# The last unit of a fused attention and feed-forward kernel: the tile of two units' rests second in its block, and another order of products and stores in the last tile

## Chip, core and metric

The kernel runs on one core of a Trainium2 chip. The metric is the device time of one execution in microseconds (us); of several runs the median is taken.

## The reference

Attention with normalized queries and keys on 8 batches of 12 heads, 448 positions and 64 channels; its output, as 3584 rows of 768, goes through a feed-forward layer of 2048 hidden units with a squared ReLU. All in fp32.

```
q_n, k_n = rmsnorm(q, g_q), rmsnorm(k, g_k)            # over the 64 channels
attn = softmax(q_n @ k_n.T / 8) @ v                    # (8, 12, 448, 64)
x = attn.transpose(0, 2, 1, 3).reshape(3584, 768)
h = np.maximum(x @ w_in, 0.0)                          # w_in (768, 2048)
out = h * h @ w_out                                    # w_out (2048, 768)
```

## The kernel before, in words

The batches are taken in pairs: a **unit** `u` is two batches of 448 rows, so there are four units, 0 to 3. While TensorE (PE) runs the feed-forward layer of one unit, the attention of the next is woven in between; the last unit, 3, has no attention beside it. `final` is true for it.

A unit's feed-forward layer (`ffn`) goes over four **blocks** (`NBLK`) of the hidden units. In each block the first matrix product gives the hidden values `hid` (`deep_products`, matmuls on L1042), and the second product (`second_products`, matmuls on L1251 and L1165) multiplies them by a part of `w_out` and adds the result to accumulators in SBUF. Both use a scheme with seven products in place of eight (Strassen's, in Winograd's form): for each tile the upper and lower rows and the left and right half of the columns are the four quarters. `PRODUCTS` lists for each of P1 to P7 which of three PSUM banks it uses, whether it starts that bank anew or adds to what an earlier product left there, and its two operands. After a product, an engine adds the bank to the quarters that it belongs to: P1 and P2 to the upper left (`c11`), P6 and P3 to the upper right (`c12`), P4 to the lower left (`c21`), P5 to the lower right (`c22`), and P7 to both lower quarters. P6 adds to P1's bank and P7 to that of P1 and P6; P3 adds to P5's bank. These additions are L1345 (`add_to`) and L1272 (P4, a subtraction) on VectorE (DVE); in a unit's first block they are copies instead, some of them on ScalarE (ACT, L1341 and L1266).

Of the 448 rows of a batch, 384 make three tiles of 128 (`NT` is 3, `tt` counts them); the tile `tt` has 128 rows of the unit's first batch as its upper rows (`accs[2 * tt]`) and 128 of its second as its lower rows (`accs[2 * tt + 1]`). The 64 **rest** rows of each batch are left. In units 0 and 3 the rests of the unit's own two batches are multiplied in `multiply_rest` (L1165). Units 1 and 2 keep the hidden values of their rests in DRAM (`keep_rests`), and the last unit brings them back block by block (`bring_rests`, loads on L1192), makes the sums that the scheme needs on GpSimd (POOL, `add_rests`, L1203), and multiplies them as one more tile with the number `NT`; its two accumulators are `extra["accs"]`, in the trace `qk`, as they lie in a room that held queries and keys before. Its hidden values are `extra[...]`, in the trace `wT`.

In a block of the last unit the tiles come in the order 0, 1, 2, `NT`. Tile 0 has the order of products `FIRST_OF_BLOCK`, which holds the rest products too; the other tiles have `SECOND_ORDER`: P1, P2, P5, P6, P4, P3, P7.

In the last block (`blk == NBLK - 1`) the accumulators are stored. `product` puts `(tt, 0)`, the upper rows, in `to_store` after P3, and `(tt, 1)`, the lower rows, after P7. `store_some` empties that list after P2 and P4 of a later tile, and what is left at the end of the last tile is stored in the loop on L1329. `store_rows` finds the accumulator and its rows in the output, `store` (L1346) issues a DMA on SyncE's queue (SP): one of 128 rows for a tile, two of 64 rows where the rows belong to rests. SP works off its queue in order, and each of its DMAs waits for the additions that it needs; other engines' order does not hold it up otherwise. In the last block SP has 12 stores: two of the unit's own rests, two each of tiles 0, 1 and 2 (in the trace `out_dram<-acc`), and four of tile `NT` (`out_dram<-qk`).

Which of two programs runs is decided at the start by a branch on L104; at its end each engine branches once more (L104) to the common end of the kernel (L1893), where SP waits for the DMAs' semaphores and all engines meet.

Of the kernel before, what the change touches and what calls it, by code (L numbers as in the profile page):

```python
# [39 lines left out]
def kernel(  # L40
# [63 lines left out]
    with tc.If(flag > 0) as either:  # L104
        program(tc, rows, v, g, wide, ones, moe_w_in, moe_w_out, out, shift=False)
    with either.Else():
        program(tc, rows, v, g, wide, ones, moe_w_in, moe_w_out, out, shift=True)
# [118 lines left out]
def program(ctx, tc, rows, v, g, wide, ones, moe_w_in, moe_w_out, out, shift):  # L226

    nc = tc.nc

    B, H, S, D = v.shape  # L230
    NPAIR = H // 2
    DM, DFF = moe_w_in.shape
# [3 lines left out]
    HALF = DM // 2  # L236
    REST = S % P
    NT = S // P
    NBLK = 4
# [666 lines left out]
    def turn_roles(*order):  # L906
        roles[:] = [roles[n] for n in order]
# [8 lines left out]
    FIRST_ORDER = ["P1", "P5", "P2", "P6", "P3", "P4", "P7"]  # L916
    FIRST_OF_BLOCK = ["P1", "rest0", "P5", "P4", "P6", "P2", "rest1", "P3", "P7"]
    SECOND_ORDER = ["P1", "P2", "P5", "P6", "P4", "P3", "P7"]
    SPLIT_ORDER = [
        ("P1", 0, 0), ("P1", 1, 3), ("P4", 0, 2), ("P5", 0, 1), ("P4", 1, 4), ("P6", 0, 0),  # L920
        ("P2", 0, 2), ("P3", 0, 1), ("P7", 0, 0), ("P6", 1, 3), ("P2", 1, 1), ("P5", 1, 0),
# [21 lines left out]
    def ffn(u):  # L943

        accs = []
        for blk in range(NBLK):

            hid = [
                ffn_p.tile([P, 2, 2, S], F32, name="hid", tag=f"hid{a}", bufs=1) for a in range(2)
            ]  # L950
            sums_ = [
                ffn_p.tile([P, 2, NT * P], F32, name="sums", tag=f"S{n}", bufs=1) for n in range(3)
            ]
            second = second_products(u, blk, hid, sums_, accs)
            if u == B // 2 - 1:
                bring_rests(blk)
                add_rests()
            if u:
                yield from deep_products(u, blk, hid, sums_, second)
            else:  # L960
                for t in range(2):
                    products = first_products(u, 2 * blk + t, [a[:, t] for a in hid])
                    for n, cost in enumerate(products):
                        if t and n < 4:
                            hidden_sum(hid, sums_, 0, n)
                        if t and blk == NBLK - 1:
                            let_go(u, PRODUCTS[FIRST_ORDER[n]][3])
                        yield cost
                make_all_deep()
                if blk == NBLK - 1:  # L970
                    for n in range(4):
                        load_piece(n, False)
                        load_piece(n, True)
            yield from second
# [184 lines left out]
    def multiply_rest(u, blk, hid, places, some, acc=None, halves=range(2)):  # L1159

        w_sb = [out_sb[n] for n in out_of(u, blk)]
        for half in halves:
            ps = places[half][:, 0:HALF]
            for a, t in some:
                nc.tensor.matmul(  # L1165
                    ps, lhsT=hid[a].rearrange("p t e s -> p t (e s)")[:, t, ds(NT * P, P)],
                    rhs=w_sb[t][:, 2 * a + half, :],
                    start=(a, t) == PARTS[0], stop=(a, t) == PARTS[-1],
                )
            if acc is not None:  # L1170
                add_to(acc[:, ts(half, HALF)], ps, blk == 0)
# [33 lines left out]
    def second_products(u, blk, hid, sums_, accs):  # L1205

        split, final = u in KEPT, u == B // 2 - 1
# [18 lines left out]
                yield len(some) * COST_OUT  # L1226
            turn_roles(2, 1, 0)

        def store_rows(tt, e):
            if tt is None or tt == NT:  # L1230
                n = u if tt is None else KEPT[e]
                parts = [(2 * n, P * NT, REST), (2 * n + 1, 0, REST)]
            else:
                parts = [(2 * u + e, REST * e + P * tt, P)]
            store(accs[-1] if tt is None else accs_of(tt)[e], parts)

        def accs_of(tt):
            return extra["accs"] if tt == NT else accs[2 * tt : 2 * tt + 2]
# [5 lines left out]
        def product(tt, name, ps, engine):  # L1244

            upper_acc, lower_acc = accs_of(tt)
            c11, c12 = [upper_acc[:, ts(h, HALF)] for h in range(2)]
            c21, c22 = [lower_acc[:, ts(h, HALF)] for h in range(2)]
            role, first, left, right = PRODUCTS[name]
            for t in range(2):  # L1250
                nc.tensor.matmul(  # L1251
                    ps, lhsT=extra[left][:, t] if tt == NT else lefts[left][:, t, ts(tt, P)],
                    rhs=w_sb[t][:, OUT.index(right), :], start=first and t == 0, stop=t == 1,
                    skip_group_check=not first,
                )
            if name == "P1":
                add_to(c11, ps, blk == 0, engine)
            elif name == "P5":
                add_to(c22, ps, blk == 0, engine)
            elif name == "P2":  # L1260
                add_to(c11, ps)
            elif name == "P6":
                add_to(c12, ps, blk == 0, engine)
            elif name == "P4":
                if blk == 0 and engine is nc.scalar:
                    nc.scalar.mul(c21, ps, -1.0)  # L1266
                elif blk == 0:
                    nc.vector.tensor_scalar(
                        out=c21, in0=ps, scalar1=-1.0, scalar2=None, op0=ALU.mult
                    )  # L1270
                else:
                    nc.vector.tensor_tensor(out=c21, in0=c21, in1=ps, op=ALU.subtract)  # L1272
            elif name == "P3":
                add_to(c12, ps)
                to_store.append((tt, 0))
            else:
                add_to(c21, ps)
                add_to(c22, ps)
                to_store.append((tt, 1))

        def sums_behind_first():
            make_sums(0, 1)
            yield COST_OUT
            make_sums(2, 3)
            held.discard("pool")

        def store_some(name):
            if name in ("P2", "P4") and blk == NBLK - 1:
                while to_store:
                    store_rows(*to_store.popleft())  # L1290

        if split:
            places = [*roles, banks[1], banks[2]]
            for name, tt, n in SPLIT_ORDER:
                engine = nc.scalar if tt and n < 3 else nc.vector
# [8 lines left out]
                if tt:  # L1304
                    store_some(name)
                yield COST_OUT
        for tt in range(0 if split else NT + final):
            order = SECOND_ORDER if tt or not u else FIRST_OF_BLOCK
            for name in order:
                if name.startswith("rest"):  # L1310
                    a = int(name[-1])
                    multiply_rest(
                        u, blk, hid, banks[2:0:-1], PARTS_BY_ROW[2 * a : 2 * a + 2],
                        accs[-1] if a else None,
                    )
                    if a:
                        held.discard("others")
                    yield 2 * COST_OUT
                    continue
                ps = roles[PRODUCTS[name][0]][:, 0:HALF]  # L1320
                product(tt, name, ps, nc.scalar if order is SECOND_ORDER else nc.vector)
                if name == "P1" and order is FIRST_OF_BLOCK:
                    yield from sums_behind_first()
                    continue
                if order is not FIRST_OF_BLOCK:
                    store_some(name)
                yield COST_OUT
            turn_roles(2, 0, 1)
        while to_store and blk == NBLK - 1:  # L1329
            some = to_store.popleft()  # L1330
            if final:
                store_rows(*some)
            else:
                later.append([2, lambda some=some: store_rows(*some)])
        for n in ns:
# [3 lines left out]
    def add_to(acc, ps, first=False, engine=nc.scalar):  # L1339
        if first and engine is nc.scalar:  # L1340
            nc.scalar.copy(acc, ps)  # L1341
        elif first:
            nc.vector.tensor_copy(out=acc, in_=ps)
        else:
            nc.vector.tensor_tensor(out=acc, in0=acc, in1=ps, op=ALU.add)  # L1345
    def store(acc, parts):  # L1346

        at = 0
        for b, row, n in parts:
            nc.sync.dma_start(out[ds(b * S + row, n), :], acc[at : at + n, :])  # L1350
            at += n


# [465 lines left out]
    with tc.manual_schedule(engines=ENGINES):  # L1819
# [8 lines left out]
        for i in range(len(pairs) + 1):  # L1828
            for n in range(1 if whole(i) else VISITS):
                at = i * VISITS + n - VISITS - unit  # L1830
# [3 lines left out]
                u, x = divmod(at, unit)  # L1834
                if x == 0:
                    u, x = u - 1, unit
# [61 lines left out]
```

## Time and profile before

| | |
|---|---|
| median of 3 runs | 1393.48 us (1393.12 to 1394.81) |
| the profiled execution, in all | 1394.38 us |
| its span, first to last instruction | 1392.6 us |
| granted TensorE clock, mean | 0.998 of full |
| PE busy with matmuls | 1363.3 us, 98% of the span |
| VectorE, ScalarE, GpSimd busy | 58%, 44%, 57% |
| DMA | 233.36 MB, mean 168 GB/s |
| matmuls L1251 on `hid`, `sums` | 768 and 576, mean 488 and 490 ns busy, some 323 ns from start to start in the last unit |
| additions L1345 on accumulators | 312 of 128x384, mean 548 ns |

Busy times of different engines lie beside each other and do not add up to the span. A matmul's busy time overlaps the next one's, so the distance from start to start says what a row of matmuls takes. In the lines of a profile the form is: source line, engine, operation, output<-input, and then counts and times; "SPq" is SyncE's instruction queue, where a DMA's time is that of its issue, and the time from issue to landing stands apart.

### The profile page before, as it was taken

What the parts mean: (1) busy time and instruction counts of PE and PEld (TensorE: products, weight loads), DVE (VectorE), ACT (ScalarE), POOL (GpSimd) and SP (SyncE); (2) the same over time, 40 slices, a digit from 0 to 9 for tenths busy, and PEclk for the clock granted to TensorE, in tenths of its full rate; (3) what the DMA queues carried; (4) which work ended last, traced back from release to release, by engine and by line L of the source; (5) the groups of instructions that cost most, each with busy time, mean ns of one, the idle gap of its engine ahead of it and who ended that gap; (6) DMA issues with size and microseconds to landing.
All of it is one profiled execution on the core that took longest, in us unless ns stands there. A gap on an engine that the chain in (4) does not pass through costs nothing.

```text
span 1392.6 us, 19474 instructions
## 1 busy us (share of the span) xinstructions
PE 1363.3 (98%) x6320; PEld 845.7 (61%) x6320; DVE 807.2 (58%) x1635; ACT 608.3 (44%) x1118; POOL 789.6 (57%) x794
## 2 busy tenths in 40 slices
PE   7999999999999999999999999999999999999997
PEld 3333444444444466676758586676768677868684
DVE  4786545867758755555556755455546642445444
ACT  6885477757666244353434244442434032202020
POOL 5668664746656868576667877566745630303030
PEclk9999999999999999999999999999999999999999
DMA  5566746968769875664739475755527442424223
GB/s 147 149 168 169 203 117 159 264 179 219 233 155 284 231 215 162 187 173 141 204 86 279 140 225 149 211 153 176 146 86 239 142 165 103 135 90 149 78 90 100
DMA packets 385588, 233.36 MB, mean 168 GB/s; under 512 B 272452, under 2 KB 354244, under 8 KB 381380
## 3 DMA queue, kind: packets, MB, share of 16 engines
q1 hardware_dynamic: 385184, 231.95, 57.7%
q8 instruction: 52, 0.85, 0.3%
q14 instruction: 60, 0.49, 0.1%
q10 hardware_dynamic: 292, 0.07, 0.0%
HBM read 174.59 MB, written 57.34 MB: 167 GB/s over the span
## 4 chain that ended last, share of the span: by engine, by line
PE 81%; POOL 4%; DVE 4%; DMA 3%; issue 3%; SPq 2%; ACT 2%; POOLq 0%; ACTq 0%; DVEq 0%
PE bank L1251 30%; PE bank L1042 20%; PE bank L986 8%; PE bank L446 5%; PE bank L536 5%; PE bank L550 4%; PE bank L435 4%; PE bank L1165 2%; POOL sum L473 2%; PE bank L585 1%; DMA qk<-in_k_dram 1%; PE bank L611 1%; SPq L326 1%; SPq L318 1%; PE bank L571 1%
## 5 line engine op out<-in xcount | busy, mean ns | idle before, releaser
L1042 PE MATMUL bank<-xT,in_sb 128*128 128x224 f32 x1344 | 289.3, 354 | 2.9 <-ACT part L1031 2.3
L1251 PE MATMUL bank<-out_sb,hid 128*128 128x384 f32 x768 | 272.5, 488 | 2.2 <-POOL out_sb L1514 1.4
L1345 DVE TENSOR_TENSOR acc<-acc,bank 128x384 f32<-128x384 f32 x312 | 166.6, 548 | 164.6 <-PE bank L1251 138.1
L1042 PEld LDWEIGHTS bank<-xT,in_sb 128*128 128x128 f32 x1344 | 252.6, 190 | 15.0 <-ACT wT L454 5.6
L454 ACT ACTIVATE wT<-bank,rr 128x448 f32<-128x448 f32 x288 | 163.5, 631 | 155.1 <-PE bank L435 92.7
L1251 PE MATMUL bank<-out_sb,sums 128*128 128x384 f32 x576 | 207.2, 490 | 1.3 <-DVE acc L1345 0.9
L1251 PEld LDWEIGHTS bank<-out_sb,hid 128*128 128x128 f32 x768 | 144.7, 190 | 104.5 <-issue 5.6
L204 POOL TENSOR_TENSOR rr<-ms,minus_half 128x8 f32<-128x8 f32 (+1 forms) x96 | 146.0, 1521 | 73.7 <-DVE ms L197 63.8
L1251 PEld LDWEIGHTS bank<-out_sb,sums 128*128 128x128 f32 x576 | 107.7, 190 | 86.3 <-issue 4.3
L1027 DVE TENSOR_TENSOR hid<-hid,bank 128x224 f32<-128x224 f32 x312 | 111.0, 383 | 83.9 <-PE bank L1042 79.1
L986 PE MATMUL bank<-xT,in_sb 128*128 128x448 f32 x336 | 131.9, 546 | 0.1
L473 POOL TENSOR_TENSOR sum<-sum,wT 128x448 f32<-128x448 f32 (+1 forms) x96 | 110.6, 1173 | 8.1 <-ACT wT L454 6.6
L986 PEld LDWEIGHTS bank<-xT,in_sb 128*128 128x128 f32 x336 | 62.1, 190 | 69.0 <-issue 60.2
L446 PE MATMUL bank<-qT,kT 64*128 64x448 f32 (+1 forms) x492 | 100.5, 571 | 1.9 <-DVE qT L409 1.1
L473 POOL TENSOR_TENSOR sum<-wT 128x448 f32<-128x448 f32 x48 | 55.8, 1183 | 69.8 <-ACT wT L454 69.8
L1099 ACT ACTIVATE hid<-hid 128x448 f32<-128x448 f32 x96 | 55.0, 573 | 66.7 <-DVE hid L1027 48.5
L435 PE MATMUL bank<-qT,kT 64*64 64x448 f32 x552 | 77.0, 547 | 1.9 <-ACT wT L454 1.9
L1042 PE MATMUL bank<-more,in_sb 128*128 128x224 f32 x288 | 76.2, 357 | 1.4 <-DVE hid L1037 1.4
L550 PE MATMUL bank<-wT,vt 64*64 64x448 f32 x576 | 74.3, 548 | 0.0
L1039 ACT COPY hid<-bank 128x448 f32<-128x448 f32 x24 | 12.8, 532 | 137.3 <-PE bank L1042 137.3
L369 ACT ACTIVATE qT<-qT,g 128x448 f32<-128x448 f32 x34 | 22.6, 665 | 113.7 <-DVE qT L367 113.7
L446 PEld LDWEIGHTS bank<-qT,kT 64*128 64x128 f32 (+1 forms) x492 | 34.9, 166 | 60.4 <-issue 36.8
(140 smaller groups left out, 2059.1 us busy)
## 6 DMA issues: line engine op xcount, KB each, us to landing
out_sb<-out_forms SPq DMA_DIRECT2D x24, 1536.0 KB, 9.9
in_sb<-in_deep SPq DMA_DIRECT2D x64, 384.0 KB, 4.2
in_sb<-in_deep SPq DMA_DIRECT2D x80, 256.0 KB, 4.1
words<-in_moe_w_in_dram SPq DMA_DIRECT2D x32, 384.0 KB, 3.8
words<-in_moe_w_out_dram SPq DMA_DIRECT2D x32, 384.0 KB, 3.6
out_forms<-out_sb SPq DMA_DIRECT2D x8, 1536.0 KB, 7.5
qk<-in_q_dram SPq DMA_DIRECT2D x96, 96.0 KB, 2.6
qk<-in_k_dram SPq DMA_DIRECT2D x96, 96.0 KB, 2.7
```

The costliest lines, as they stand in the source:

```text
L204: self.nc.gpsimd.tensor_tensor(out=self.rr[i][:, x, 0 : self.count(i)], in0=ms, in1=self.minus_half.to_broadcast(list(ms.shape)), op=ALU.pow,)
L435: nc.tensor.matmul(sc[ds(half * D, D)], lhsT=turned[i, 1][ds(e * D, D), ds(m * P + half * D, D)], rhs=turned[i, 0][ds(e * D, D), :], start ...
L446: nc.tensor.matmul(sc[some], lhsT=turned[p, 1][r, keys], rhs=turned[p, 0][r, :], start=True, stop=True,)
L454: nc.scalar.activation(new_weights((i, m), e), sc, AF.Exp, scale=rows.rr[i][:, 1, 2 * m + e : 2 * m + e + 1],)
L473: nc.gpsimd.tensor_tensor(out=sums[i, e][some], in0=left[some], in1=weights[key_of(i, m), e][some], op=ALU.add)
L536: nc.tensor.matmul(values_bank(i)[ds(e * D, D), :], lhsT=lasts[i % 2][mine, e, :] if m == NJ else values[i][:, m, e, :], rhs=weights[key_o ...
L550: nc.tensor.matmul(bank[ds(e * D, D), :], lhsT=values[i][keys, n, e, :], rhs=weights[(i, n), e][keys], start=n == 0, stop=n == NJ - 1 and ...
L986: nc.tensor.matmul(ps, lhsT=w_sb[:, IN.index(left), c, :], rhs=forms[u, c][right], start=first and c == 0, stop=c == NK - 1, skip_group_ch ...
L1027: nc.vector.tensor_tensor(out=quarter(name, n), in0=quarter(base, n), in1=ps, op=ALU.add)
L1042: nc.tensor.matmul(ps, lhsT=left, rhs=right, start=start, stop=stop, skip_group_check=True)
L1251: nc.tensor.matmul(ps, lhsT=extra[left][:, t] if tt == NT else lefts[left][:, t, ts(tt, P)], rhs=w_sb[t][:, OUT.index(right), :], start=fi ...
L1345: nc.vector.tensor_tensor(out=acc, in0=acc, in1=ps, op=ALU.add)
```

## The change

In the last unit the tiles of every block come in the order 0, `NT`, 1, 2, so that the tile of the two units' rests is second and tile 2 is last. In the last block, tile 2 has a new order, `LAST_ORDER`, with P7 ahead of P3. There the upper rows are stored in two parts: the left half of the columns after P2, the right half at the end. The lower rows, complete after P7, stand before that right half on SP's queue. `store` and `store_rows` take the columns as an argument. The last block's stores are then 13, and the last three of them are those of tile 2: left half of the upper rows, lower rows, right half of the upper rows. Every other product, addition and load is the same, in the same numbers.

```
+    LAST_ORDER = ["P1", "P2", "P5", "P6", "P4", "P7", "P3"]
...
-        def store_rows(tt, e):
+        def store_rows(tt, e, columns=slice(None)):
...
-            store(accs[-1] if tt is None else accs_of(tt)[e], parts)
+            store(accs[-1] if tt is None else accs_of(tt)[e], parts, columns)
...
-        for tt in range(0 if split else NT + final):
-            order = SECOND_ORDER if tt or not u else FIRST_OF_BLOCK
+        for tt in () if split else (0, NT, 1, 2) if final else range(NT):
+            ends = final and blk == NBLK - 1 and tt == NT - 1
+            order = LAST_ORDER if ends else SECOND_ORDER if tt or not u else FIRST_OF_BLOCK
...
-                product(tt, name, ps, nc.scalar if order is SECOND_ORDER else nc.vector)
+                product(tt, name, ps, nc.vector if order is FIRST_OF_BLOCK else nc.scalar)
...
                 if order is not FIRST_OF_BLOCK:
                     store_some(name)
+                if ends and name == "P2":
+                    store_rows(tt, 0, slice(0, HALF))
...
         while to_store and blk == NBLK - 1:
             some = to_store.popleft()
             if final:
-                store_rows(*some)
+                store_rows(*some, slice(0 if some[1] else HALF, DM))
...
-    def store(acc, parts):
+    def store(acc, parts, columns=slice(None)):
...
-            nc.sync.dma_start(out[ds(b * S + row, n), :], acc[at : at + n, :])
+            nc.sync.dma_start(out[ds(b * S + row, n), columns], acc[at : at + n, columns])
```

## The prediction

> **What bounds the kernel now.** I read the page's first part, then the table of stretches over the last unit (its four blocks end near 1166, 1237, 1307 and 1376 us, each followed by its last tile), then the timeline of the last microseconds, then what the stores and the ending branch did.
>
> The page's first part and the table of stretches. In the table the columns after the length are busy us and count of each engine, the granted clock, the DMA share and GB/s:
>
> ```profile
> PE 1363.3 (98%) x6320; PEld 845.7 (61%) x6320; DVE 807.2 (58%) x1635; ACT 608.3 (44%) x1118; POOL 789.6 (57%) x794
> ```
>
> ```profile
> 1096.00:1166.00 70.00, 70.00 (x281) 52.92 (x280) 31.54 (x68) 17.68 (x36) 23.68 (x26) 1.00 0.39 136
> 1307.00:1376.00 69.00, 69.00 (x279) 52.38 (x278) 32.21 (x67) 12.47 (x25) 15.84 (x16) 1.00 0.30 111
> 1376.00:1393.00 17.00, 9.07 (x29) 5.01 (x27) 5.37 (x10) 0.00 (x0) 0.00 (x0) 0.91 0.32 96
> ```
>
> PE is busy for 70.00 of 70.00 and 69.00 of 69.00 us: up to its last product the unit is a gapless row of matmuls. A new order cannot make that row shorter, only open holes in it. What is left is the stretch after PE's last product, some 7.5 us (1385.1 to 1392.6). The timeline of it:
>
> ```profile
> 1375.88 9.19 PE L1251 MATMUL bank<-out_sb,wT 128*128 128x384 f32 x28
> ...
> 1383.82 0.56 DVE L1345 TENSOR_TENSOR qk<-qk,bank 128x384 f32<-128x384 f32 x1 [0.74 <-PE bank L1251]
> 1384.40 3.58 SPq L1350 DMA_DIRECT2D out_dram<-qk  x4
> 1385.11 1.02 DVE L1345 TENSOR_TENSOR qk<-qk,bank 128x384 f32<-128x384 f32 x2 [0.73 <-PE bank L1251]
> ```
>
> The last tile is the one of the two rests; P7 comes last and has two additions (1.02 us) behind it. Both halves of its rows leave by four DMAs, two of them only after the second addition. Narrow windows on the stores give the last two apart (issue time min/median/max in ns):
>
> ```profile
> L1350 SPq DMA_DIRECT2D out_dram<-qk x1: 466/466/466, 1386.2 to 1386.2; - x1
> ...
> L1350 SPq DMA_DIRECT2D out_dram<-qk x1: 1307/1307/1307, 1386.7 to 1386.7; - x1
> DMA to landing us min/median/max: 3.6/3.6/3.6
> ```
>
> The last store is issued from 1386.67 to 1387.98 and lands 3.6 us after its start, at 1390.3. What stands after it, by source line (L104 is the branch that leaves the program, L1893 the common end):
>
> ```profile
> L104 DVEq COMPARE_BRANCH  x1: 57/57/57, 1385.1 to 1385.1; - x1
> L104 SPq COMPARE_BRANCH  x1: 43/43/43, 1388.0 to 1388.0; - x1
> ```
>
> ```profile
> L1893 SPq EVENT_SEMAPHORE  x4: 28/28/28, 1391.2 to 1391.4; - x4
> L1893 ACTq DRAIN  x1: 81/81/81, 1350.5 to 1350.5; - x1
> L1893 DVEq DRAIN  x1: 57/57/57, 1388.6 to 1388.6; - x1
> ```
>
> SP branches at 1388.0 and does nothing until 1391.2, 0.9 us after the last store has landed. So it is the branch that ends the kernel, not the landing: SP's last issue, 3.2 us of branch, then 1.35 us of closing semaphores to 1392.6. DVE needs 3.5 us for the same branch, ACT, which left while the DMA engines were idle, 2.5 us (1348.0 to 1350.5).
>
> [...] after SP's branch two packets of the instruction queue are seen at about 1389.6 and nothing of SP before 1391.2. [...] the trace has 553 (mean of the seven additions on qk). [...] Here SP's 128-row stores of that size land in 2.3 us when alone; the four 64-row stores of half the size, close together, take 3.2 to 4.0. I use the trace's values.
>
> **The change part by part.**
>
> *Order of tiles, four blocks.* A tile is 7 products of 4 matmuls; the row of x28 above occupies PE from 1375.88 to 1384.91, 9.03 us, as the other tiles do (1357.82, 1366.85, 1375.88). Nothing is added or removed: 0 us on PE if the inputs are there. The tile of the rests is wanted 18.06 us earlier. Its sums are POOL's L1203: in block 0 the four are done at 1111.3 (last start 1110.5 plus 0.76), wanted at 1146.05 (its old 1164.11 less 18.06), 35 us spare; in block 3 done at 1320.1 (last start 1319.4), wanted at 1357.8, 38 us spare. The loads L1192 of the next block wait for this tile's reads, with load_piece and load_out behind them on SP's queue; the wait ends 18 us sooner, so nothing behind it is later. POOL's 104.4 us of waiting for these loads lie in idle time. Without the covers of 35 us the tile would stall PE by what is missing. Tile 2 now borders on the next block, whose first ACT and DVE writes into `hid` wait for its reads; but they need results of matmuls that stand behind those reads on PE: 0.
>
> *Last tile, P7 before P3.* P7 adds into P6's bank with only P4 between. The addition of a product ends 0.2 + 0.56 us after the product's last matmul starts (1383.62, 1383.82 to 1384.38); P7 would start 1.29 + 0.32 us after it: 0.85 us spare, 0. P3's bank was read three products earlier. Now one addition (P3's) follows PE's last product instead of two: it runs 1385.11 to 1385.66 in place of 1386.13. **-0.47 us.**
>
> *Stores.* Twelve DMAs become thirteen; the added one (upper rows, left half, issued after P2's addition at about 1378.5) meets an idle SP, 0.33 to 0.6 us by the issues of the page's 8 acc stores: 0. The rests' and tile 1's stores all leave one or two tiles earlier. P7's two additions end at 1384.84 (1383.82 plus 1.02); the lower rows' store is issued then, free again at about 1385.2. The right half waits for P3's addition and starts at 1385.69 (0.03 after it, as at 1386.16 now). One last store instead of two: **-0.51 us** (1386.16 to 1386.67). Its issue: now 1.31 us, and a packet of 16 KB of the instruction queue starts at the same moment, 1.5 us after DVE's branch; that would still be near 1386.7, and SP would be done by then. The 128-row stores took 0.33 us alone and up to 0.50 in a series; the form of 128 rows by 1.5 KB is not in the stores of before. Bounds 0.33 and 1.31; I take 0.40: **-0.91 us**. SP then branches at 1386.1 in place of 1388.0.
>
> *Branch and end.* With 3.2 us the semaphores start at 1389.3, the end is 1390.7. Less than half as many bytes are under way at that time (the lower rows' 384 KB from 1384.87 and 192 KB, against 768 KB after 1384.4), so the fetch should wait less: between 0 and 0.7 us (3.2 less ACT's 2.5); I take **-0.2 us**. The right half lands, by 2.3 to 3.6 us, between 1388.0 and 1389.3, before SP looks. DVE's end of branch at 1388.6 is not late either, since SP is needed at the same barrier after it.
>
> Sum: -0.47 - 0.51 - 0.91 - 0.2 = **-2.1 us**: the profiled span goes from 1392.6 to 1390.5. That execution took 1394.38 in all, 1.8 around the span, and stands 0.9 above the median of the runs, 1393.48. From the median: **1391.4 us**.
>
> A difference of 0.2% is 2.8 us here, about what a measurement of this kernel can tell from no change (its three runs lie 1.7 us apart). The forecast is 0.15%.
>
> **The rivals.**
> - *The gain is bigger.* The branch takes ACT's 2.5 us and the issue 0.33: -0.47 - 0.51 - 0.98 - 0.7 = -2.7 us, and with the before runs' upper half (1394.38, 1394.81) as the truer level the comparison shows -2.8 to -3.3. For it: the fetch now falls after most of the stores' bytes. Against: DVE's branch took 3.5 us with half of the stores under way. 1390.5 us. Chance 0.25.
> - *The gain is small.* DVE's fetch meets the last issue after all (1.31 us again), or the right half in 1.5 KB rows lands last, at 4.0 us or more (1389.7 and later), and the landing takes the branch's place: -0.5 to -1.2 us, 1392.6. Against: the new issue should end 0.6 us before that fetch. Chance 0.12. That the stores would not be issued ahead at all is no case: the built order of SP's instructions has left half, lower rows, right half as its last three.
> - *Slower.* At each of three block borders PE stops because tile 2's `hid` and `sums` are read to the very end, where the tile of the rests used to give 9.03 us of cover. Price: as long as one 128x448 ACT or DVE step (0.58 to 1.1 us) each, times three, 1.7 to 3.3 us, against a saving of 2.1; it decides from 0.7 us a border on, and to end beyond +0.2% it would need 1.6. Against: [...] 70.00 of 70.00 us busy shows that no border stops it now. 1394.5 us, up to 1396.5. Chance 0.03.
>
> The forecast has the remaining 0.60, itself -1.5 to -2.6 us. Chances: faster by over 0.2% 0.25, within 0.72, slower 0.03. Range: 1390.2 (the bigger gain) to 1393.0 (the small one).
>
> **What would show it.** Right: the blocks' stretches still 70.00 of 70.00; PE's last matmul, now on `sums`, at the same 1384.6; one addition of 0.56 us after 1385.1; SP's last store near 1385.7 with 0.3 to 0.5 us of issue; SP's first L1893 near 1389.1; span near 1390.5. Wrong: idle PE before L1042 at 1166, 1237 or 1307; idle PE at 1357.8 with a releaser on POOL; a last issue of over 1 us; semaphores of L1893 that stand apart because a landing is awaited.

## The result and the profile after

The changed kernel takes 1391.94 us (median of 20 runs, 1389.98 to 1394.52), the kernel before 1393.99 us (1392.60 to 1396.41) in runs beside it: ratio 0.9984, 95% interval [0.9977, 0.9991], so 0.16% or 2.2 us less. The forecast was 1391.4 us and 0.15%.

The profiled execution has a span of 1389.3 us, 3.3 us under the one before. Only 2.0 of these belong to the change. In the trace the 2001st matmul, some 590 us ahead of the last unit, starts at 507.5 us in place of 508.6, and the first addition behind PE's last product at 1383.86 in place of 1385.11: most of that lead of 1.25 us was there long before anything that was changed. So I count from that addition on and call the stretch to the span's end the **tail**: 7.47 us before, 5.46 us after. The same stretch is the measure in the experiments, from one trace each. Three pairs of kernels below end in nearly the same way and differ in it by 0.01 us (6.12 and 6.11), 0.08 (3.58 and 3.50) and 0.20 (5.46 and 5.66), so I read nothing into steps smaller than that.

The table of stretches over the last unit, columns as before: PE is as gapless as it was.

```profile
1096.00:1166.00 70.00, 70.00 (x281) 52.91 (x280) 30.98 (x66) 17.78 (x36) 26.52 (x30) 1.00 0.41 143
1307.00:1376.00 69.00, 69.00 (x279) 52.37 (x278) 32.70 (x68) 12.49 (x25) 12.98 (x12) 1.00 0.31 109
1376.00:1393.00 17.00, 7.82 (x25) 4.29 (x23) 4.35 (x8) 0.00 (x0) 0.00 (x0) 0.90 0.20 73
```

The timeline at the end of the last tile: P7's two additions come first, one addition stands alone behind PE's last product.

```profile
1382.37 1.45 PE L1252 MATMUL bank<-out_sb,sums 128*128 128x384 f32 x4
...
1382.57 1.02 DVE L1349 TENSOR_TENSOR acc<-acc,bank 128x384 f32<-128x384 f32 x2 [0.73 <-PE bank L1252]
1383.86 0.55 DVE L1349 TENSOR_TENSOR acc<-acc,bank 128x384 f32<-128x384 f32 x1 [0.27 <-PE bank L1252]
```

The last store in a narrow window on the output: one issue of 332 ns where the last of before took 1307, but a landing that takes 3.9 us.

```profile
L1354 SPq DMA_DIRECT2D out_dram<-acc x1: 332/332/332, 1384.4 to 1384.4; - x1
...
DMA to landing us min/median/max: 3.9/3.9/3.9
```

The branches (L104), and the common end (now L1897), by source line:

```profile
L104 DVEq COMPARE_BRANCH  x1: 57/57/57, 1383.9 to 1383.9; - x1
L104 SPq COMPARE_BRANCH  x1: 43/43/43, 1384.8 to 1384.8; - x1
```

```profile
L1897 SPq EVENT_SEMAPHORE  x8: 17/28/28, 1387.9 to 1388.4; - x8
L1897 DVEq DRAIN  x1: 57/57/57, 1387.6 to 1387.6; - x1
```

SP branches 1.0 us after the start of the last addition, not 2.9, and is back 3.0 us later (3.15 before). The tail, step by step, in us from the start of the first addition behind the last product; "leaves" is the end of SP's branch instruction, "back" its first instruction at the common end:

| | last store issued | its issue | SP leaves | SP back | end |
|---|---|---|---|---|---|
| before | 1.56 | 1.31 | 2.97 | 6.12 | 7.47 |
| after | 0.58 | 0.33 | 1.00 | 4.03 | 5.46 |

### The profile page after: what moved, and what is told of

The parts are those of the page before. It is cut to its first block, busy times and chain, and to the rows that moved or that the text cites. A ratio compares the mean times of both kernels' runs of the same rounds, so it can differ in the third digit from the quotient of the medians.

```text
span 1389.3 us, 19475 instructions
## 1 busy us (share of the span) xinstructions
PE 1361.8 (98%) x6320; PEld 845.1 (61%) x6320; DVE 807.2 (58%) x1635; ACT 608.9 (44%) x1118; POOL 789.9 (57%) x794
## 4 chain that ended last, share of the span: by engine, by line
PE 82%; DVE 5%; POOL 5%; issue 2%; DMA 2%; SPq 2%; ACT 1%; DVEq 0%; POOLq 0%; ACTq 0%
PE bank L1252 30%; PE bank L1043 20%; PE bank L987 8%; PE bank L446 5%; PE bank L536 5%; PE bank L550 4%; PE bank L435 4%; PE bank L1166 2%; POOL sum L473 2%; PE bank L585 1%; DMA qk<-in_k_dram 1%; PE bank L611 1%; PE bank L571 1%; PE bank L602 1%; SPq L159 1%
## 5 line engine op out<-in xcount | busy, mean ns | idle before, releaser
L1096 POOL TENSOR_TENSOR hid<-hid 128x448 f32<-128x448 f32 x24 | 27.2, 1138 | 122.9 <-DVE hid L1028 118.1
```

## The experiments

**The tiles alone.**

```
-            ends = final and blk == NBLK - 1 and tt == NT - 1
+            ends = False
...
-                store_rows(*some, slice(0 if some[1] else HALF, DM))
+                store_rows(*some)
```

> Only the order of tiles is changed (0, rests, 1, 2); products keep P3, P7 at the end and the stores stay whole. The measure is the tail: from the start of the first addition behind the last product to the end of the span, 7.47 us in the kernel before and 5.46 in the changed one. Theory (SP's last issue and the ending branch set the end): two additions stand before the last store, but it is one DMA of 128 rows in place of two of 64, so tail 1.05 + 0.35 + 3.1 + 1.4 = about 5.9 us, some 1.5 us less than before, ratio 0.9989. Rival (the new order of products and the split stores make the gain): tail about 7.4 us, ratio 1.000. Rival (the moved tile makes the row of matmuls itself shorter): idle PE that goes from the blocks, or PE's row from the unit's start to its last product shorter by over 0.5 us.

Measured: ratio 0.9989 [0.9983, 0.9996], tail 6.12 us, near the theory's 5.9; SP leaves at 1.47, is back at 4.77. From the first matmul of the rests' tile in block 0 to the last matmul it is 238.54 us, as in the changed kernel; in the kernel before 220.48, and with the two tiles by which that first matmul has moved (18.06 us) 238.54 again. So PE's row is the same to 0.01 us. Two thirds of the gain come without the new order of products, by one store behind the last addition in place of two (by the tails, 1.35 of 2.01 us).

**Products and stores alone**, in the rests' tile, which stays last.

```
-            ends = final and blk == NBLK - 1 and tt == NT - 1
+            ends = final and blk == NBLK - 1 and tt == NT
...
-        for tt in () if split else (0, NT, 1, 2) if final else range(NT):
+        for tt in range(0 if split else NT + final):
```

> The order of tiles stays (the rests' tile last), and that last tile gets P7 before P3 and its stores in left half, lower rows, right half, each as two DMAs of 64 rows. Theory: the two issues of the lower rows (0.47 + 0.59) keep SP until 0.85 us after the start of the last addition, the right half's two issues follow, so SP leaves at about 1.9 us (2.7 if the last issue is again 1.3 us): tail 6.5 us, or 7.2. Rival (one addition less and an earlier start are what counts): tail 5.9 us or less. Ratio to before 0.9993 by the theory.

Measured: ratio 0.9994 [0.9985, 1.0002], tail 6.36 us. SP's issues queue up as worked out: four in a row, 0.47 to 0.59 us each, the last from 1.56 to 2.15 us, SP leaves at 2.24. The last one starts where the 1.31 us issue of before did, and takes 0.59: the 16 KB packet of the instruction queue begins at 2.10 here, not at 1.57.

**The upper rows whole.** The left half is not stored ahead; the last store has 384 KB.

```
-                if ends and name == "P2":
-                    store_rows(tt, 0, slice(0, HALF))
...
-                store_rows(*some, slice(0 if some[1] else HALF, DM))
+                store_rows(*some)
```

> The changed kernel without the split: the upper rows of the last tile are stored whole (384 KB) after P3, behind the lower rows. Theory one (issue and branch alone set the end, the split does nothing): tail 5.5 us as in the changed kernel. Theory two (in the changed kernel the last landing, 3.9 us after its issue, is already level with the branch): the landing comes 0.5 to 0.9 us later and is waited for, tail 5.9 to 6.3 us.

Measured: ratio 0.9992 [0.9985, 0.9998], tail 5.88 us. The size of theory two, but by another way than it said. SP leaves at 1.00 us as in the changed kernel and is back only at 4.45, not at 4.03. By source line, the branch and the end:

```profile
L104 SPq COMPARE_BRANCH  x1: 43/43/43, 1386.4 to 1386.4; - x1
```

```profile
L1895 SPq EVENT_SEMAPHORE  x8: 17/28/28, 1389.9 to 1390.5; - x8
L1895 DVEq DRAIN  x1: 58/58/58, 1389.2 to 1389.2; - x1
```

It is the branch that takes 3.45 us. The landing is waited for too (it comes at 4.85 us and costs SP 0.09 us), but that is the smaller part.

**The last store in two.**

```
+            if two:
+                parts = [(b, row + n // 2 * x, n // 2) for b, row, n in parts for x in range(2)]
...
-                store_rows(*some, slice(0 if some[1] else HALF, DM))
+                store_rows(*some, slice(0 if some[1] else HALF, DM), not some[1])
```

> The changed kernel with its last store (right half of the upper rows) as two DMAs of 64 rows in place of one of 128. Theory (each issue counts): one issue of 0.47 and one of 0.59 in place of 0.33, SP leaves 0.73 us later, tail 6.2 us; if the second issue meets DVE's instruction fetch it is 1.3 us and the tail 6.9. Rival (the landing of all stores sets the end): tail within 0.2 us of 5.46, since the bytes are the same.

Measured: ratio 0.9998 [0.9990, 1.0005], tail 5.79 us. SP leaves 0.79 us later (1.79), as the theory says, yet is back only 0.42 later (4.45): its branch takes 2.66 us. Neither side is right: not each issue counts in full, for the branch that starts later here finds more of the stores' bytes gone. Counted in the DMA packets, 184 KB of the stores begin after SP leaves here, 408 KB in the changed kernel. The times are worse than this one trace explains (it would give 0.9988, just below the interval's lower edge); that stays open.

**The programs swapped.**

```
-        program(tc, rows, v, g, wide, ones, moe_w_in, moe_w_out, out, shift=False)
+        program(tc, rows, v, g, wide, ones, moe_w_in, moe_w_out, out, shift=True)
     with either.Else():
-        program(tc, rows, v, g, wide, ones, moe_w_in, moe_w_out, out, shift=True)
+        program(tc, rows, v, g, wide, ones, moe_w_in, moe_w_out, out, shift=False)
```

with the flag's comparison turned round (`is_gt` for `is_le`).

> The changed kernel with the two programs in the other order (the one for large gains in the If, the one that runs in the Else), so that the program that runs stands last, right before the common end, and the far jump comes at the start. Theory (the ending branch with its fetch of instructions is what follows SP's last issue): SP is in the closing semaphores at once, the last store lands without the fetches' packets at about 2.6 to 2.9 us after the start of the last addition, tail about 3.9 us in place of 5.46; the jump at the start costs from 0 to 3 us, so ratio to before 0.997 to 0.9995. Rival (the landings or the closing barrier set the end): tail still 5.3 to 5.5 us.

Measured: tail 3.58 us, and yet ratio 1.0026 [1.0015, 1.0038]. The end shows what the branch costs. Its lines in narrow windows, the common end and then the last store:

```profile
L1897 SPq EVENT_SEMAPHORE  x10: 17/28/28, 1394.4 to 1396.9; - x10
```

```profile
L1354 SPq DMA_DIRECT2D out_dram<-acc x1: 332/332/332, 1394.0 to 1394.0; - x1
...
DMA to landing us min/median/max: 2.0/2.0/2.0
```

No branch, no packet of instructions in the tail, SP at the end's semaphores 0.04 us after its issue, and the same store lands in 2.0 us, not 3.9. The price at the start was expected at 0 to 3 us and is more, and with it the expected ratio failed: the 21st matmul comes 2.9 us later than in the kernel before (17.4 for 14.5), the 801st 5.7 (163.4 for 157.7), the 3001st 8.1 (699.6 for 691.5; the other kernels lie between 688.0 and 691.5). The first 2.9 us fit the far jump at the start: DVE branches at 10.2 us and its next operation comes at 13.28, in the changed kernel at 10.50 after a branch at 10.3; what adds the rest through the attention part isn't settled.

**No branch at all.** The program for large gains is left out; for other inputs than these it would be needed.

```
-    flag = nc.values_load(bounded, min_val=0, max_val=1)
-    with tc.If(flag > 0) as either:
-        program(..., shift=False)
-    with either.Else():
-        program(..., shift=True)
+    program(..., shift=False)
```

> The changed kernel without the If: the program for large gains is left out, and with it the load of the flag and both branches. Theory: tail about 3.9 us as with the swapped programs, and no jump at the start, so the whole is at least 1.5 us shorter than the changed kernel: ratio to before 0.9973 or less. Rival (the end is set by landings or the barrier): tail 5.3 to 5.5 us, any gain lies at the start.

Measured: ratio 0.9970 [0.9958, 0.9982], tail 3.50 us; the last store lands at 2.60 us, and the end follows 0.90 later. It beats both kernels, but not as the same function. The gain over the changed kernel (0.14% by the two ratios, 2.0 us) is that of its tail (1.96 us), though six runs leave about 1.7 us on either side. At the start no price of the branch that isn't taken is seen: the 21st matmul starts at 14.35 us here, and between 14.28 and 14.62 in the twelve kernels that have that branch and don't take it.

**P3 in halves, one bank.**

```
+            if name == "P3" and u == B // 2 - 1 and blk == NBLK - 1 and tt == NT - 1:
+                for some in (slice(0, HALF // 2), slice(HALF // 2, HALF)):
...
+                    add_to(c12[:, some], ps[:, some])
+                store_rows(tt, 1)
+                to_store.clear()
+                for n in range(2):
+                    store_rows(tt, 0, slice(HALF + HALF // 2 * n, HALF + HALF // 2 * (n + 1)))
+                return
```

> The changed kernel with the last product (P3 of the last tile) as two column halves of 192, each with its own addition and its own store, so that only an addition of 128x192 and a store of 96 KB stand behind the last matmul. Theory: the last addition takes 0.36 us in place of 0.56, SP leaves 0.2 us earlier, tail about 5.25 us; the four shorter matmuls lengthen PE's row by about 0.1 us. Ratio to before 0.9983, not to be told from the changed kernel by its times, only by the trace. Rival (the branch's fetch waits for the stores' bytes): tail shorter by 0.4 us or more, as fewer bytes stand ahead of it.

Measured: ratio 0.9986 [0.9978, 0.9994], tail 4.84 us, but PE's row is 1.00 us longer, not the 0.1 that I had estimated. The timeline of PE:

```profile
1383.08 0.81 PE L1254 MATMUL bank<-out_sb,sums 128*128 128x192 f32 x4
1384.62 0.92 PE L1254 MATMUL bank<-out_sb,sums 128*128 128x192 f32 x4 [0.73 <-DVE acc L1363]
```

The second half waits for the addition of the first, as both lie in one bank. That was the step I had missed; it takes back more than the tail gave. The shorter addition takes 0.35 us; the expected 0.36 lies on the line through the 0.39 of 224 columns and the 0.56 of 384 in the kernel before. The tail's 0.62 us is three times the 0.20 that this addition saves: the branch takes 2.70 us with fewer bytes ahead of it (132 KB begin after SP leaves, not 408), as the rival has it. In good part that is the stall's own doing, for the lower rows' store is issued 1.25 us ahead of the last addition here, and 0.24 in the changed kernel.

**Small last stores.** The lower rows and the right half are written in 16 columns each; the rest of them is left out.

```
-                store_rows(*some, slice(0 if some[1] else HALF, DM))
+                store_rows(*some, slice(0, 16) if some[1] else slice(HALF, HALF + 16))
```

> The changed kernel with the last two stores cut to 16 columns each (the rest of the lower rows and of the right half is not written). Theory (SP's fetch of instructions waits behind the stores' bytes in the DMA engines): from SP's branch to its next instruction 2.5 us, as for ACT in the kernel before, in place of 3.0, and tail 4.9 us. Rival (the branch takes its time whatever is under way): 3.0 us and tail 5.3 to 5.5.

Measured: ratio 0.9984 [0.9978, 0.9990], tail 5.06 us; from SP's branch (1.00) to its return (3.72) 2.72 us, between the theory's 2.5 and the rival's 3.0. So the stores' bytes cost some 0.3 us of the branch in the changed kernel; 2.7 us it takes even when hardly a byte is under way (8 KB begin after SP leaves). Even this store lands only 3.1 us after its issue. The trace records the landing of a store in 16 parts: 14 are there at 2.00 us after the addition's start, the last at 3.70; a 16 KB packet of instructions ran from 1.21 to 2.62.

**The kernel before, rests in one store.**

```
-                parts = [(2 * n, P * NT, REST), (2 * n + 1, 0, REST)]
+                parts = [(2 * n, P * NT, P)]
```

> The kernel before with one edit: the 64 rest rows of the first batch and of the second stand behind each other in the output, so a store of rests is one DMA of 128 rows in place of two of 64. Tiles and products as before. Theory (the number of issues behind the last addition, and their form, make most of the gain; which tile is last makes none): two additions, then one issue of 0.33 us, so tail 6.1 us as with the tiles moved alone, ratio 0.9989. Rival (the place of the tile matters in itself): tail over 7 us, ratio 1.000.

Measured: tail 6.11 us, ratio 0.9994 [0.9987, 1.0002]. One line in the kernel before, and its tail is that of the tiles moved alone (6.12), with SP leaving at 1.47 us in both. The last store in a narrow window:

```profile
L1350 SPq DMA_DIRECT2D out_dram<-qk x1: 332/332/332, 1385.1 to 1385.1; - x1
```

The times hold both no gain and the expected 0.9989 just within the interval.

**Products and stores, rests in one store.** The second experiment with that line.

> Tile order as before (rests last), the new order of products and the split stores in that tile, and its stores as one DMA of 128 rows each. Theory: the tail of the changed kernel, 5.4 to 5.6 us, in place of the 6.36 us with stores of 64 rows, and its whole gain, ratio 0.9984, without moving a tile. Rival (the moved tile has a part in it): tail or PE's row longer by 0.3 us or more than in the changed kernel.

Measured: tail 5.66 us, ratio 0.9986 [0.9980, 0.9993]: the changed kernel's gain with no tile moved. SP leaves at 1.00 and is back at 3.93 us; the 0.2 us above the changed kernel come of its wait of 0.40 us for the last landing (4.44 us), which stands earlier among the end's semaphores here. In this kernel the landing, and not the branch, ends last.

**The last product in two banks.** P5 and P3 of the last tile in halves of two matmuls each, the right half in a free bank; the rests' tile in one store as above.

```
+                for n, some in enumerate(pieces_):
+                    room = (banks[3] if n else ps)[:, 0 : HALF // 2]
...
+                    add_to(acc[:, some], room)
+                    if not first:
+                        at = HALF + HALF // 2 * n
+                        store_rows(tt, 0, slice(at, at + HALF // 2))
```

> The changed kernel, stores of rests in one DMA, and in the last tile P5 and P3 in two column halves of 192, this time in two PSUM banks, so that no half waits for the addition of the other. Theory: PE's row is again of the changed kernel's length within 0.1 us (eight half matmuls of 0.16 us for four of 0.32), the last addition takes 0.35 us and the last store is 96 KB: tail 4.8 to 4.9 us as with the halves in one bank, so the whole is about 0.6 us shorter than the changed kernel, ratio to before 0.998. Rival (halves cost PE time in themselves): PE's row longer by 0.6 us or more, and nothing gained.

Measured: PE's row is the changed kernel's within 0.02 us, so the two banks mend that. But the ratio is 0.9990 [0.9981, 0.9998], the tail 6.73 us and not 4.8 to 4.9. The last two stores in a narrow window:

```profile
L1373 SPq DMA_DIRECT2D out_dram<-acc x2: 383/1123/1863, 1385.3 to 1385.8; - x2
```

The last issue took 1.86 us. It started at 0.65 us, and a 16 KB packet of the instruction queue at 0.77. The 1.31 us issue of before had met such a packet too (1.56 and 1.57). In the views of the DMA queues (packets, MB, share of the 16 engines' time) it is the one of q8, an instruction queue, first in a window on this kernel's last issue, then in one on that of before:

```profile
q8 instruction: 1, 0.02, 5.1%
```

```profile
q8 instruction: 1, 0.02, 11.6%
```

All traces together, counted packet by packet, bear this out. In the 14 traces 446 stores go to the output; these two alone had such a packet begin in their first 0.13 us, and these two alone took over 1 us to issue. Of all of SP's DMAs, 95 had one begin in their first 0.13 us: 67 of them took over 1 us, while of the other 17403 it was 6%. When the packet began 0.2 to 0.4 us after the issue's start, 4 of 102 did.

**Two banks, one last store** of 192 KB after both additions; so its issue is over before such a packet.

```
-                    if not first:
-                        at = HALF + HALF // 2 * n
-                        store_rows(tt, 0, slice(at, at + HALF // 2))
+                if not first:
+                    store_rows(tt, 0, slice(HALF, DM))
```

> As the kernel with the last product in two banks, but with one store of the right half (192 KB) after both additions, so that the last issue starts at 0.38 us after the start of the last addition in place of 0.65. Theory (the issue of 1.86 us there was its meeting with a 16 KB instruction packet that began at 0.77 us): the issue takes 0.33 us and is over by 0.72, SP leaves at 0.76, tail 4.8 to 5.2 us, the whole 0.3 to 0.6 us shorter than the changed kernel, ratio to before 0.998. Rival (short additions or two banks lengthen the last issue in themselves): issue again over 1 us, tail 6 us or more.

Measured: ratio 0.9987 [0.9980, 0.9993], tail 5.38 us, a little over the expected 4.8 to 5.2. The issue takes 0.33 us again:

```profile
L1372 SPq DMA_DIRECT2D out_dram<-acc x2: 332/332/332, 1382.7 to 1383.4; - x2
```

So neither the banks nor the short additions lengthen it. But SP, which leaves at 0.81, is back at 4.04 us as in the changed kernel (4.03): its branch takes 3.23 us. The earlier start is lost in a longer branch: the lower rows' store, issued at the same time as in the changed kernel, is still on its way, and 489 KB of the stores begin after SP leaves, not 408. An earlier last issue bought nothing here that one trace could show.

## Why the prediction was right

- **PE's row, all tile moves: 0.** Shown, by 70.00 of 70.00 us and by 238.54 us three times (tiles alone, after, and before with the 18.06 added).
- **P7 before P3: no stall, one addition less, -0.47.** Right: the last addition ends at 0.55 us in place of 1.02.
- **One last store instead of two, -0.51.** Right: with the addition it makes 0.98 us (1.56 to 0.58). Shown apart by the kernel before with the rests in one store.
- **The last issue, -0.91.** Measured -0.98 (1.31 to 0.33). That a packet of instructions makes such an issue slow rests on two meetings (1.31 and 1.86 us), on 64-row stores of the same place that met none at their start and took 0.59 (products and stores alone, last store in two), on the count over all traces, and on the last experiment, which moved the issue out of the way. It is no fixed rule: 27 of the 95 issues that met one took 0.56 us or less.
- **Whose packet that is.** The prediction took it for DVE's fetch, 1.5 us after DVE's branch; no trace names a packet's owner, but the traces speak against this reading and for PE's own instructions. In the kernel before, one such packet comes for 255 of PE's instructions on average (50 gaps of 185 to 329; between the two behind PE's branch lie 12). In the twelve kernels that branch at the end, two follow PE's branch, the second 0.73 to 1.99 us after that branch ends; with P3 in halves PE's branch ends only at 3.58 us, and the second packet moves to 4.31. DVE's return follows a packet of 8 KB, by 1.82 to 1.88 us in all twelve. In the other eleven the 16 KB packet begins between 0.77 and 2.23 us, so that the changed kernel's issue (0.58 to 0.91) would miss it was less sure than the prediction had it.
- **The branch, -0.2.** Measured -0.13 (3.15 to 3.02), but not for the reason given, so the size was luck. The prediction reads 384 KB and 192 KB as less than half of 768; they are three quarters. And as SP branches 2 us earlier, more of the bytes are still to come: 408 KB of the stores begin after it leaves, 225 KB before the change. The step is also near what one trace can tell: the kernel with products and stores and the rests in one store has the same stores at the same times, and its branch takes 2.92 us where the changed kernel's takes 3.02.
- **That the branch and not the landing sets the end.** Right for the kernel before. The swapped programs and the kernel without a branch show what it costs: 1.9 us of tail go with it. There the landing, which comes at 2.60 us without the fetches, ends last. In the twelve kernels that branch at the end, SP's branch took 2.66 to 3.45 us. In the kernel before, two 8 KB packets of the instruction queue begin at 4.48 and 4.60 us, 1.5 and 1.6 us after SP leaves, and SP is back at 6.12; in the swapped programs there is no such packet in the tail and SP goes on after 0.04 us. That the packets bring the instructions behind the branch and SP waits for them, the "fetch" of this document, is my reading of that; no trace says what a packet holds. In the changed kernel the landing is level with it, as the next point shows.
- **"The right half lands before SP looks."** Missed by little: 3.9 us from issue to landing, not 2.3 to 3.6, and SP waited 0.09 us for it. 14 of 16 parts were there at 2.86 us, the last two at 3.52 and 4.49. The step that failed took the lower bound from 128-row stores of 384 KB that met no fetch (2.3 us) and the upper one from the last store of before; without a fetch the same store lands in 2.0 us. This wait is the +0.08 us that the sum lacks: -0.47 - 0.51 - 0.98 - 0.13 + 0.08 = -2.01.
- The rival of a bigger gain fell as ACT's 2.5 us of branch in the kernel before, with two packets of the instruction queue and nothing else on the DMA engines from 1346 to 1351 us, were out of reach even for small stores (2.7); its argument, that the fetch falls after most of the stores' bytes, doesn't hold, with 408 of 576 KB to come. That of a small gain fell as the issue met no packet; its other half came close, a landing of 3.9 us where it named 4.0. That of a slower kernel fell as no border of blocks shows idle PE.

The place of the tile was not what made the gain. It was needed for it only because the rests' tile is stored in four pieces. With one line in `store_rows` for that, the kernel before has two thirds of the gain by its tail, though its times (0.9994) don't rule out that it gains nothing; and the new products and stores reach the changed kernel's ratio with the tiles in their old order.

## What to carry to other kernels

When the engine that bounds a kernel is gapless, look behind its last instruction: write down in a row the last addition, each DMA issue, the jump and the landings, and change what stands in that row. Let the last product feed one addition and one store, in as few DMAs and bytes as can be: here one DMA in place of two behind the last addition took 1.36 us from the tail (7.47 to 6.11), and a last store of 192 KB in place of 384 took 0.42 (5.88 to 5.46). Read from a fixed event on, a trace told steps of 0.3 us and more here, where twenty runs leave 1 us on either side. If the last instruction issued is followed by a jump, price that too: here it cost about as much as the change gained, 1.9 of 2.0 us.

## What the hardware showed that I had not expected

- In these 14 traces a DMA issue on SP mostly took 1.3 to 2.1 us when a 16 KB packet of the instruction queue began in its first 0.13 us (67 of 95 issues), and 0.33 to 0.38 for the 128-row stores of the last tile that met none there.
- Stores and instruction fetches held each other up here. SP's taken branch took 2.66 to 2.79 us where 8 to 184 KB of stores began after SP left, and 3.45 with 603 KB; between, the order isn't strict (3.15 with 225 KB, 2.78 with 258). What varies is the time from SP's leaving to the second 8 KB packet of instructions in the tail, 0.88 to 1.81 us; from the start of that packet SP was back in 1.58 to 1.91 us. And one or two of a store's 16 parts landed up to 2.2 us after the others in the tails with fetches, while without them all 16 landed within 0.2 us. The last store of the changed kernel landed in 3.9 us, and in 2.0 with the programs swapped.
- A product in two column halves in one PSUM bank stopped PE for the first half's addition (1.00 us in all); in two banks PE's row was the changed kernel's within 0.02 us.
- A program that is reached by a jump at the start ran longer by more than the jump: 2.9 us at once and over 8 us by its middle, in one trace. Why is open.
